# A transformer block with a hand-written order per engine: more warm-up matmuls, two weight corrections moved to ScalarE, and a new order

## The chip, the cores and the metric

The kernel runs on one core of a Trainium2 chip. The metric is device microseconds of one execution. A run is also profiled once: the hardware profiler records every instruction of one execution, and its "span" is the time from the first to the last instruction.

## The reference

One block on x of 2048 rows and 640 columns, in bfloat16: linear attention with 32 heads of 20 columns, then a gated bilinear layer.

```python
q, k, v = split(layernorm(x) @ wqkv)             # 32 heads, Dh = 20
pq = q @ w_phi[h];  pk = k @ w_phi[h]            # 20 x 20 per head
phi_q = concat(softmax(pq), softmax(-pq))        # 40 per head
phi_k = concat(softmax(pk), softmax(-pk))
kv = phi_k^T @ v;  z = sum over rows of phi_k
o = (phi_q @ kv) / (phi_q @ z + 1e-6)
h = x + o @ wo
h2 = h + ((layernorm(h) @ w_gate) * (layernorm(h) @ w_up)) @ w_down
```

## The kernel before, in words

The 2048 rows are 16 tiles of 128. The program is built by a small recorder (`Prog`): every operation names its engine, the regions that it reads and writes, and a unit such as k7. The table `ORDER` (L58 to L107) then gives, for each of PE, DVE, ACT, POOL and SP (the queue that issues DMAs), the sequence of units. Each engine executes its operations strictly in that sequence. `place()` (L205) walks the five lists with planner costs (`t`, `lat`, `at`) to choose buffers and to count semaphores; the costs set no time on the chip and do not change an engine's sequence. Most matmuls write one of four PSUM buffers, so a matmul group also waits until an earlier group's buffer has been read.

The units that matter here, with PE's work and what follows it:

- **warm** (L576): 30 matmuls of 128 columns on a constant, which have no use as arithmetic.
- **wk** (L676): for each of the five row blocks of the key weights, five matmuls of one column (column sums of the weights, for their means) and five transposes through PE. The blocks arrive by three loads: block 0, blocks 1 and 2 (both on SP), blocks 3 and 4 (on ACT's queue). DVE then makes the negative means (L689, `nmean`), POOL spreads them over a tile (L691), and DVE and ACT add them to the transposed blocks (L716, L713).
- **x0 to x4** (L743 to L752): key weights times `Phi`, a band matrix that holds w_phi, in six matmuls each (twice for x0 and x1: once on the raw weights, once on the spread means). DVE builds three fifths of `Phi` (L552) and POOL the rest. ACT (L763) or DVE (L766) copies the product to `Wp`. These are the key weights of all later steps.
- **s0, s2, s4, s8, s12**: row sums and row sums of squares for the layernorm of tiles 0 to 1, 2 to 3, 4 to 7 and so on, from PE; DVE (L613, L617) takes them out of PSUM, POOL makes the scales (`rs`). For s12 ACT takes the squares (L565).
- **wv, c0 to c4**: the sums of the value weights, and DVE's subtraction of their mean (L785).
- **wm, wq0 to wq4, y0 to y4**: the same for the query weights. `lwq` loads the weights, t0 to t4 load their five column blocks transposed (`WT[:, 0]`) by DMA; wm (L726) makes the means on PE and ACT (L730, `nmeanq`); wq (L734) adds the negative means to each of the five blocks, on DVE; y (L737) multiplies by `Phi`.
- **k, v, q**: projections of a tile, ten matmuls of 320 columns each. For a key tile DVE takes the absolute maximum (L815), scales it (L818), ACT does two exponentials (L822); K: DVE sums and inverts (L833, L835), POOL divides (L836). For q the steps are alike (Q: L855, L860, L861, L866), with a transposing DMA behind them.
- **A0 to A14**: kv of two tiles each; **Aout**: DVE takes kv out of PSUM (L902, L905).
- **n, h, f, d, e**: per tile the numerator and division (n), the output projection (h), and per block of four tiles the gated layer up (f) and down (d, e). For tiles 0 and 1 the transposes in n and h go through PE and ACT (L482, L485), for the others by DMA.

The loads of SP's list are called lT (x transposed), lx (x as it is), lwq, lwo, lg, lu, ld.

Of the kernel before, what the change touches and what calls it, by code (L numbers as in the profile page):

```python
# [7 lines left out]
ACT = mybir.ActivationFunctionType  # L8
ALU = mybir.AluOpType
# [38 lines left out]
NRAW = 2  # L48
# [8 lines left out]

ORDER = {  # L58
# [14 lines left out]
    "DVE":  # L73
# [12 lines left out]
    "ACT":  # L86
# [9 lines left out]
    "POOL":  # L96
# [10 lines left out]
}  # L107
# [270 lines left out]
def _build(ctx, nc, A_x, A_wqkv, A_w_phi, A_wo, B_w_gate, B_w_up, B_w_down, out):  # L378
    g = Prog(nc, ctx)
# [43 lines left out]
    nmeanq = sb([P, NC], FP32, "nmeanq")  # L423
# [9 lines left out]
    WT = pq[:, NC * D:3 * NC * D].rearrange("p (w a n) -> p w a n", w=2, a=NC)  # L433
# [18 lines left out]
    R_Wnat, R_WT, R_Phi = regs(NC), [regs(NC), regs((NRAW + 1) * NC)], regs(NC)  # L452
    R_Wp = [regs(NC) for _ in range(3)]
    R_Wrows, R_G, R_id, R_one = Reg(), regs(NC), Reg(), Reg()
    R_Wo, R_Wgu, R_Wd = regs(NC), regs(2), Reg()
    R_wsum, R_nmean, R_nmu, R_nmuk = regs(NC), regs(NC), Reg(), Reg()
# [38 lines left out]
    def U(name):  # L495
        g.unit = name
# [3 lines left out]
    def load_wnat(w, cs=(0, NC), eng="SP", at=0.0):  # L500
        c0, c1 = cs
        load(Wnat[:, c0:c1, :], A_wqkv[P * c0:P * c1, D * w:D * (w + 1)].rearrange("(c p) n -> p c n", p=P), R_Wnat[c0:c1],
             0.3 * (c1 - c0), eng=eng, at=at)
# [8 lines left out]
        load(Wp[:, c0:c1, 2 * D:3 * D], A_wqkv[P * c0:P * c1, 2 * D:3 * D].rearrange("(c p) n -> p c n", p=P), R_Wp[2][c0:c1], 0.16 * (c1 - c0), at=at)  # L512

    U("in")
    load_wnat(1, (3, 5), "ACT", at=4.8)
    load(Wrows[:, :, :], A_w_phi.rearrange("h d f -> (h d) f").rearrange("(a p) f -> p a f", p=P), [R_Wrows], 0.03, eng="ACT", at=5.5)
    load_wnat(1, (0, 1), at=2.9)
    load_wnat(1, (1, 3), at=4.7)
    load_xT(0, 5.35)
    load_xT(1, 5.95)  # L520
    load_wv(0, 5, 9.15)
    for t, at in ((2, 8.95), (3, 9.55)):
        load_xT(t, at)


# [21 lines left out]
    for a in range(NC):  # L547
        lo, hi = CH[a]
        n = hi - lo + 1
# [26 lines left out]
    def warm(n):  # L576
        v = Buf(p_ps, 2)
        one = nc.const_aps.tensor(1.0, (P, P), BF16)
        g.op("PE", lambda e: mms(e, [(PS[v.i][:, 0, 0:P], one, one, True, True) for _ in range(n)]),
             wr=v.R, use=[v], t=0.1 * n, lat=0.1 * n + 0.15)  # L580

# [60 lines left out]
    def wk_rounds():  # L642
        vr, vt = Buf(p_ps, 2), Buf(p_ps, 2)
# [12 lines left out]
        def turn(c):  # L656
            def f(e):
                ins = None
                for a in range(NC):
                    o_ = raw(c)[:, a, :] if c < NRAW else late(a, P * (c - NRAW), P * (c - NRAW + 1))  # L660
                    ins = e.transpose(out=o_, in_=Wnat[:, c, P * a:P * (a + 1)], identity=ident[:, :])  # L661
                return ins
            g.op("PE", f, rd=[R_Wnat[c], R_id], wr=[vr.R[c]] if c < NRAW else vt.R + [vr.R[0]], use=[vr] if c < NRAW else [vt, vr], t=0.28, lat=0.43)

        def means(c):
            v = vx[1]
# [18 lines left out]
        for c in range(NC):  # L685
            U("wk")
            means(c)
            if c == NC - 1:
                g.op("DVE", lambda e: e.tensor_scalar(out=nmean[:, :], in0=PS[vx[1].i][:, 1, MC:MC + NC], scalar1=-1.0 / SC, scalar2=None,  # L689
                                                      op0=ALU.mult), rd=[R_mean], wr=R_nmean, use=[vx[1]], t=0.08, lat=0.2)  # L690
                g.op("POOL", lambda e: e.tensor_copy(nmuk[:, :, :], nmean[:, :].unsqueeze(2).to_broadcast([P, NC, P])), rd=R_nmean,  # L691
                     wr=[R_nmuk], t=0.85, lat=0.95)
# [33 lines left out]
    def wq_means():  # L726
        U("wm")
        v = Buf(p_ps, 2)
        g.op("PE", lambda e: mms(e, mean_mms(PS[v.i][:, 0, :], range(NC), 0)), rd=R_Wnat + [R_one], wr=v.R, use=[v], t=0.64, lat=0.79)
        g.op("ACT", lambda e: e.activation(out=nmeanq[:, :], in_=PS[v.i][:, 0, 0:NC], func=ACT.Copy, scale=-1.0 / SC),  # L730
             rd=[v.R[0]], wr=[R_nmu], use=[v], t=0.1, lat=0.23)
        for a in range(NC):
            U("wq%d" % a)
            g.op("DVE", lambda e, a=a: e.tensor_scalar(out=WT[:, 0, a, :], in0=WT[:, 0, a, :], scalar1=nmeanq[:, a:a + 1], scalar2=None,  # L734
                                                       op0=ALU.add), t=0.35, lat=0.47, rd=[R_nmu, R_WT[0][a]], wr=[R_WT[0][a]])

    def wq_round(i):  # L737
        U("y%d" % i)
# [290 lines left out]
        transpose(lambda: WT[:, 0, a, :], lambda: A_wqkv[:, P * a:P * (a + 1)], [], [R_WT[0][a]], t=1.5, size=0.75, lat=2.75)  # L1029

    U("warm")
    warm(30)
    U("wk")
    wk_rounds()
    for t in range(4, NT):
# [77 lines left out]
```

## Time and profile before

| | us |
|---|---|
| time, median of 3 (280.88 to 282.19) | 281.85 |
| the profiled execution's own time | 281.99 |
| its span | 280.3 |
| PE busy | 275.5 |
| DVE busy | 166.5 |
| ACT busy | 133.6 |
| POOL busy | 107.5 |

Busy time of PE is modelled and runs from the first to the last matmul of a dense stream, so a stall of some 0.1 to 0.3 us between two matmuls of a stream does not show as idle time. It shows in the starts: a group of ten matmuls of 320 columns that follows another starts 1.36 us after it when nothing waits. The timeline gives a start, a duration and a count for each merged group; the idle time in brackets is that of the engine just before the group, with what ended it.

### The profile page before, as it was taken

The numbers are of one execution on the slowest core, as the hardware profiler recorded it, in microseconds if no ns is written. First come the engines' busy times: TensorE is split into PE (matmuls) and PEld (weight loads), VectorE is DVE, ScalarE is ACT, GpSimd is POOL, SyncE is SP. The second block draws the span as 40 slices with busy tenths as digits, with TensorE's granted clock in tenths as the row PEclk, the third lists the DMA queues.
The fourth block names the chain that finished last, engine by engine and source line by source line (L and its number), as shares of the span: only waits on it lengthen the run. The fifth ranks groups of instructions, "written<-read, shape, count | busy, mean of one in ns | idle before, by whom it ended". The sixth has DMA issues, their size and how long they took to land.

```text
span 280.3 us, 5482 instructions
## 1 busy us (share of the span) xinstructions
PE 275.5 (98%) x2231; PEld 187.3 (67%) x2231; DVE 166.5 (59%) x316; ACT 133.6 (48%) x227; POOL 107.5 (38%) x158
## 2 busy tenths in 40 slices
PE   7999999999999999999999999999999999999996
PEld 7967777678868888877756555776454444447773
DVE  2699999999999987588446654404250323324011
ACT  2449998999746564413754513113144224340132
POOL 6636689999823240052140822240300000250151
DMA  7999800149844537978734022446411000000112
GB/s 186 283 239 179 174 4 2 24 104 287 339 96 94 93 75 198 240 114 197 101 79 110 26 47 48 117 96 73 116 23 26 0 0 0 2 23 23 49 47 70
DMA packets 65192, 28.06 MB, mean 100 GB/s; under 512 B 55696, under 2 KB 63888, under 8 KB 65168
## 3 DMA queue, kind: packets, MB, share of 16 engines
q1 hardware_dynamic: 64240, 27.37, 43.4%
q10 hardware_dynamic: 928, 0.35, 0.5%
q8 instruction: 17, 0.28, 0.4%
q14 instruction: 7, 0.06, 0.1%
HBM read 11.82 MB, written 2.62 MB: 52 GB/s over the span
## 4 chain that ended last, share of the span: by engine, by line
PE 96%; DMA 2%; DVE 0%; ACT 0%; SPq 0%; issue 0%
PE ps L572 95%; DMA phiqT<-in_A_wqkv_dram 2%; PE ps L661 1%; PE ps L482 0%; DVE outb L1019 0%; ACT phik L485 0%; SPq L467 0%
## 5 line engine op out<-in xcount | busy, mean ns | idle before, releaser
L572 PE MATMUL ps<-phik,Wgu 128*128 128x512 bf16 (+1 forms) x600 | 107.3, 336 | 0.0
L572 PEld LDWEIGHTS ps<-phik,Wgu 128*128 128x128 bf16 x600 | 58.2, 98 | 43.5 <-DVE phik L978 1.8
L572 PE MATMUL ps<-Wp,xT 128*128 128x320 bf16 x480 | 69.6, 299 | 0.0
L978 DVE TENSOR_TENSOR phik<-ps,gate 128x512 bf16<-128x512 f32 (+1 forms) x60 | 33.9, 578 | 55.6 <-PE ps L572 50.7
L572 PE MATMUL ps<-vaug,phik 128*128 128x320 bf16 (+3 forms) x544 | 60.1, 270 | 0.0
L572 PEld LDWEIGHTS ps<-Wp,xT 128*128 128x128 bf16 x480 | 45.6, 98 | 18.3 <-ACT phik L822 0.5
L976 ACT ACTIVATE gate<-ps 128x512 bf16<-128x512 f32 (+1 forms) x60 | 29.6, 511 | 58.0 <-PE ps L572 40.2
L572 PEld LDWEIGHTS ps<-vaug,phik 128*128 128x128 bf16 x544 | 43.7, 97 | 15.7
L994 POOL TENSOR_TENSOR outb<-t,x_all 128x640 bf16<-128x640 f32 x12 | 16.8, 1396 | 58.0 <-ACT t L991 49.9
L836 POOL TENSOR_TENSOR phik<-phik,Rk 128x1280 bf16<-128x1280 bf16 x16 | 37.4, 2361 | 3.4 <-DVE nb L818 3.4
L991 ACT ACTIVATE t<-ps,mh,rs 128x640 f32<-128x640 f32 x12 | 10.6, 883 | 37.7 <-PE ps L572 37.7
L815 DVE TENSOR_REDUCE ps<-ps 128x1 f32<-128x640 f32 x32 | 25.9, 817 | 1.1 <-PE ps L572 1.0
L855 DVE TENSOR_REDUCE Sq<-eq 128x64 f32<-128x1280 bf16 x16 | 23.5, 1476 | 2.8 <-ACT eq L822 2.7
L822 ACT ACTIVATE eq<-ps,nb,rs 128x640 bf16<-128x640 f32 x16 | 14.1, 884 | 19.7 <-DVE nb L818 13.6
L833 DVE TENSOR_REDUCE Ssum<-phik 128x64 f32<-128x1280 bf16 x16 | 23.2, 1461 | 0.0
L861 POOL TENSOR_TENSOR rq<-Sq,rq 128x32 f32<-128x32 f32 x16 | 4.0, 253 | 47.2 <-DVE rq L860 47.2
L961 POOL TENSOR_SCALAR vpe<-shc 128x1 f32<-128x1 f32 x16 | 3.0, 190 | 45.8 <-ACT junk L565 44.7
L866 POOL TENSOR_TENSOR eq<-eq,rq 128x640 bf16<-128x640 bf16 x16 | 20.2, 1269 | 0.9
L565 ACT ACTIVATE junk<-x_all 128x640 bf16<-128x640 bf16 x20 | 14.6, 733 | 4.4 <-DVE x_all L955 4.4
L822 ACT ACTIVATE phik<-ps,nb,rs 128x640 bf16<-128x640 f32 x16 | 14.2, 885 | 3.3 <-DVE nb L818 3.1
L936 DVE RECIPROCAL rden<-ps 128x32 f32<-128x32 f32 (+1 forms) x18 | 5.6, 324 | 14.7 <-PE ps L572 14.5
L842 ACT ACTIVATE vaug<-ps,rs 128x640 bf16<-128x640 f32 x16 | 12.8, 798 | 3.0 <-PE ps L572 2.9
(85 smaller groups left out, 247.0 us busy)
## 6 DMA issues: line engine op xcount, KB each, us to landing
x_all<-in_A_x_dram SPq DMA_DIRECT2D x4, 640.0 KB, 5.1
out_dram<-outb SPq DMA_DIRECT2D x15, 160.0 KB, 1.8
Wgu<-in_B_w_up_dram SPq DMA_DIRECT2D x1, 1920.0 KB, 9.4
Wgu<-in_B_w_gate_dram SPq DMA_DIRECT2D x1, 1920.0 KB, 15.0
vaug<-in_B_w_down_dram SPq DMA_DIRECT2D x1, 1920.0 KB, 10.3
Wp<-in_A_wqkv_dram SPq DMA_DIRECT2D x1, 800.0 KB, 5.1
phiqT<-in_A_wqkv_dram SPq DMA_DIRECT2D x1, 800.0 KB, 5.3
Wo<-in_A_wo_dram SPq DMA_DIRECT2D x1, 800.0 KB, 4.9
```

The source lines that it names most:

```text
L565: g.op("ACT", lambda e: e.activation(out=junk[:, v.i, :], in_=in_, func=func, accum_out=acc), rd=rd, wr=wr, use=[v], t=0.73, lat=0.97)
L572: ins = e.matmul(o_, lhsT=l_, rhs=r_, start=s_, stop=p_, skip_group_check=True)
L815: g.op("DVE", lambda e: e.tensor_reduce(out=mx(), in_=PS[v.i][:, :, 0:HALF], axis=AX.XY, op=ALU.max, apply_absolute_value=True, negate=Tru ...
L822: g.op("ACT", lambda e, s=s, sc=sc: e.activation(out=signed(dst(), s), in_=PS[v.i][:, :, 0:HALF].rearrange("p b (h f) -> p b h f", f=DH), ...
L833: g.op("DVE", lambda e: e.tensor_reduce(out=Ssum[:, vs.i, :], in_=x, axis=AX.X, op=ALU.add), rd=R_phik[t], wr=vs.R, use=[vs], t=1.39, lat=1.5)
L836: g.op("POOL", lambda e: e.tensor_tensor(out=x, in0=x, in1=Rk[:, vr.i, :].unsqueeze(2).to_broadcast([P, 2 * H, DH]), op=ALU.mult), rd=vr.R ...
L842: g.op("ACT", lambda e: e.activation(out=vaug[:, t, :, 0:DH].rearrange("p (b h) d -> p b h d", b=2), in_=PS[v.i][:, :, 0:HALF].rearrange(" ...
L855: g.op("DVE", lambda e: e.tensor_reduce(out=Sq[:, vs.i, :], in_=eq[:, b.i, :].rearrange("p (g f) -> p g f", f=DH), axis=AX.X, op=ALU.add), ...
L866: return e.tensor_tensor(out=x, in0=x, in1=rq[:, vr.i, :].unsqueeze(2).to_broadcast([P, H, DH]), op=ALU.mult)
L976: g.op("ACT", lambda e: e.activation(out=gate[:, vg.i, 0:P * n], in_=PS[v.i][:, 0, 0:P * n], func=ACT.Copy), rd=[v.R[0]], wr=vg.R, use=[v, ...
L978: g.op("DVE", lambda e: e.tensor_tensor(out=hhT[:, hb, ft, sl], in0=PS[v.i][:, 1, 0:P * n], in1=gate[:, vg.i, 0:P * n], op=ALU.mult), rd=[ ...
L994: g.op("POOL", lambda e: e.tensor_tensor(out=outb[:, vo.i, :], in0=t32[:, v3.i, :], in1=x_all[:, t, :], op=ALU.add), rd=v3.R + [R_h[t]], w ...
```

## The change

`warm(30)` becomes `warm(38)`. Of the five additions of the query weights' means, a = 1 and a = 3 become an ACT activation (Identity with a bias) in place of a DVE addition. Planner costs and due times change (not shown beyond one line). `ORDER` is new up to about the end of the first up-layer block; from there (q12 on PE) it is as before.

```diff
-    warm(30)
+    warm(38)
...
+            if a in (1, 3):
+                g.op("ACT", lambda e, a=a: e.activation(out=WT[:, 0, a, :], in_=WT[:, 0, a, :], func=ACT.Identity, bias=nmeanq[:, a:a + 1]),
+                     t=0.66, lat=0.8, rd=[R_nmu, R_WT[0][a]], wr=[R_WT[0][a]])
+                continue
...
-            g.op("PE", f, rd=[R_Wnat[c], R_id], ... t=0.28, lat=0.43)
+            g.op("PE", f, rd=[R_Wnat[c], R_id], ... t=0.54 if c < 3 else 0.28, lat=0.6 if c < 3 else 0.43)
```

The start of each engine's list, before (-) and after (+), cut where the lists go on:

```diff
 PE
-warm wk wk wk wk wk wk wk wk wk wk x1 s0 s0 x0 x0 x3 x2 x1 wv wv x4 k0 s2 k0 k0 s2 k0 k0 k3 k1 v2 k2 s4 s4 s4 s4 k7 v1 v3 wm k4 v4 k6 v7 y1
+warm wk wk wk wk wk wk wk wk wk s0 wk s0 x1 x1 x3 wv wv x2 x0 x0 s2 s2 x4 k0 k0 k0 k0 k0 k3 k2 wm k1 v1 s4 s4 s4 s4 k6 k4 v5 v0 k7 y3
 PE, around Aout
-A8 A10 A8 A12 A10 A12 A14 A14 q4 n1 n0 n0 n1 q7 n1 n0 h1 h0 n2 q6 h0 h1 n3 q8
+A6 A8 A8 A10 A10 A12 A14 A12 A14 n1 n0 n0 n1 q7 n1 q4 n0 h1 h0 n2 q6 h0 h1 n3 q8
 DVE
-wk in in in wk wk wk wk s0 s0 s0 x3 x1 c1 c3 c0 s2 k0 s2 s2 k0 c4 c2 k3 K0 k3 k1 K0 k2 k1 s4 s4 k2 s4 s4 s4 K3 k7 K3 k7 K1 K2 k4 K2 k4 wq4 wq1 wq0 wq2 wq3
+wk in wk in in wk wk wk s0 x1 s0 x3 s0 c4 c0 c2 s2 c1 s2 s2 k0 k0 c3 k3 k2 k3 K0 k2 k1 K3 k1 s4 s4 s4 s4 s4 wq2 k6 K3 k4 k6 K1 k4 wq0 K1 wq4
 ACT
-in in in wk wk wk x0 x2 x4 k0 k0 v2 k3 k3 k1 k1 k2 k2 v1 s12 wm v3 k7 k7 s12 v4 k4 k4
+in in in wk wk wk x2 x0 x4 k0 k0 wm k3 k3 k2 k2 v1 k1 k1 wq3 wq1 k6 k6 v0 v5 k4 k4
 POOL, the keys' divisions
-K3 K0 K1 K2 K4 K7 ... K6 K5 ... K9 ... K8 K10 K11 K13 K12 K14 K15
+K3 K1 K0 K6 K2 K4 ... K7 ... K5 ... K10 K8 K14 K9 K11 K13 K12 K15
 SP
-in x7 lx3 lT4 lT6 lT5 lT7 lwq t0 t2 t3 t4 lT8 t1 lwo lT10 lT14 lT9 lT12 lT11 lT15 lT13 Q1 Q0 lx0 Q0 Q1 lu lg
+in x7 lwq lT6 lT5 lT4 t2 lT7 t3 t1 t0 t4 lx3 lT11 lT10 lT8 lT9 lT15 lT14 lT12 lT13 lu lwo Q1 Q0 Q0 Q1 lx0 lg
```

More of the change, by code (lines that the diff above doesn't have):

```diff
@@ L514, in _build @@
     U("in")
-    load_wnat(1, (3, 5), "ACT", at=4.8)
+    load_wnat(1, (3, 5), "ACT", at=4.3)
     load(Wrows[:, :, :], A_w_phi.rearrange("h d f -> (h d) f").rearrange("(a p) f -> p a f", p=P), [R_Wrows], 0.03, eng="ACT", at=5.5)
     load_wnat(1, (0, 1), at=2.9)
-    load_wnat(1, (1, 3), at=4.7)
+    load_wnat(1, (1, 3), at=5.05)
     load_xT(0, 5.35)
@@ L521, in _build @@
     load_wv(0, 5, 9.15)
-    for t, at in ((2, 8.95), (3, 9.55)):
+    for t, at in ((2, 9.1), (3, 9.8)):
         load_xT(t, at)
@@ L579, in warm @@
         g.op("PE", lambda e: mms(e, [(PS[v.i][:, 0, 0:P], one, one, True, True) for _ in range(n)]),
-             wr=v.R, use=[v], t=0.1 * n, lat=0.1 * n + 0.15)
+             wr=v.R, use=[v], t=0.107 * n, lat=0.107 * n + 0.15)
     def stats(i0, n):
@@ L662, in f @@
                 return ins
-            g.op("PE", f, rd=[R_Wnat[c], R_id], wr=[vr.R[c]] if c < NRAW else vt.R + [vr.R[0]], use=[vr] if c < NRAW else [vt, vr], t=0.28, lat=0.43)
+            g.op("PE", f, rd=[R_Wnat[c], R_id], wr=[vr.R[c]] if c < NRAW else vt.R + [vr.R[0]], use=[vr] if c < NRAW else [vt, vr], t=0.54 if c < 3 else 0.28,
+                 lat=0.6 if c < 3 else 0.43)
         def means(c):
@@ L733, in wq_means @@
             U("wq%d" % a)
+            if a in (1, 3):
+                g.op("ACT", lambda e, a=a: e.activation(out=WT[:, 0, a, :], in_=WT[:, 0, a, :], func=ACT.Identity, bias=nmeanq[:, a:a + 1]),
+                     t=0.66, lat=0.8, rd=[R_nmu, R_WT[0][a]], wr=[R_WT[0][a]])
+                continue
             g.op("DVE", lambda e, a=a: e.tensor_scalar(out=WT[:, 0, a, :], in0=WT[:, 0, a, :], scalar1=nmeanq[:, a:a + 1], scalar2=None,
-                                                       op0=ALU.add), t=0.35, lat=0.47, rd=[R_nmu, R_WT[0][a]], wr=[R_WT[0][a]])
+                                                       op0=ALU.add), t=0.55, lat=0.67, rd=[R_nmu, R_WT[0][a]], wr=[R_WT[0][a]])
     def wq_round(i):
```

64 rows, old and new, of the table ORDER are left out of this document.

## The prediction, made before the run

> **What bounds the kernel now.** I read the page first, then the windows, then the chain in order of time.
>
> ```profile
> PE 275.5 (98%) x2231; PEld 187.3 (67%) x2231; DVE 166.5 (59%) x316; ACT 133.6 (48%) x227; POOL 107.5 (38%) x158
> PE 96%; DMA 2%; DVE 0%; ACT 0%; SPq 0%; issue 0%
> ```
>
> PE bounds the whole kernel: the chain that ends last is 96% PE. So a microsecond that PE loses anywhere is lost at the end, and one that it saves counts only if no other engine makes it wait afterwards. The windows (busy time of PE, weight loads, DVE, ACT, POOL, then granted clock) show who could:
>
> ```profile
> 0.00:10.00 10.00, 8.51 (x102) 8.28 (x103) 3.01 (x10) 3.24 (x5) 5.22 (x27) 1.00 0.90 229
> 20.00:40.00 20.00, 19.96 (x208) 15.21 (x207) 19.92 (x42) 18.59 (x30) 13.13 (x13) 1.00 0.76 137
> 20.00:70.00 50.00, 49.96 (x494) 37.43 (x493) 49.52 (x96) 46.81 (x76) 42.46 (x39) 1.00 0.52 112
> ```
>
> From 20 to 70 us DVE is full, ACT 94% and POOL 85%, with most of POOL's idle time before 40. So the change can gain in the first 10 us, where PE is idle or slow, and it can lose anything behind them, where DVE is as full as PE.
>
> **The start, step by step.** The timeline of the first 13 us:
>
> ```profile
> 0.83 3.36 PE L572 MATMUL ps<-const-bfloat16-1.0 128*128 128x128 bf16 x30 [0.83 <-PEq L1098]
> 3.98 0.32 PE L572 MATMUL ps<-ones,phiqT 128*128 128x1 bf16 x5
> 5.51 0.29 PE L572 MATMUL ps<-ones,phiqT 128*128 128x1 bf16 x5 [0.66 <-DMA phiqT<-in_A_wqkv_dram]
> 5.71 1.20 DVE L552 TENSOR_TENSOR Phi<-Wrows,G 128x140 bf16<-128x140 bf16 x3 [0.33 <-DMA Wrows<-in_A_w_phi_dram]
> 7.67 0.69 PE L661 MATMUL ps<-ident,phiqT 128*128 128x128 bf16 x5
> 7.84 0.17 DVE L689 TENSOR_SCALAR nmean<-ps 128x5 f32<-128x5 f32 x1 [0.93 <-PE ps L572]
> 8.15 0.81 PE L572 MATMUL ps<-Phi,phiqT 128*128 128x140 bf16 x6
> 8.40 1.07 DVE L716 TENSOR_SCALAR phiqT<-ps,nmean 128x384 bf16<-128x384 bf16 x3 [0.39 <-PE ps L661]
> 8.75 1.13 PE L572 MATMUL ps<-xT 128*128 128x129 bf16 x10
> 9.72 0.48 PE L572 MATMUL ps<-Phi,phiqT 128*128 128x140 bf16 x6
> 10.03 0.48 PE L572 MATMUL ps<-Phi,outb 128*128 128x140 bf16 x6
> 13.07 0.43 PE L572 MATMUL ps<-Wp,xT 128*128 128x320 bf16 x2
> ```
>
> Thirty warm-ups take 3.98 - 0.83 = 3.15 us, 0.105 each. Eight more put the first wk round at 4.82. The chain gives a round's pace:
>
> ```profile
> 1.25 4.22 DMA phiqT<-in_A_wqkv_dram
> 6.36 0.11 PE ps L572 x5
> 6.47 0.56 PE ps L661 x5
> ```
>
> A round is 0.11 + 0.56 = 0.67 us, so the first ends at 5.49, and the second round's data lands at 1.25 + 4.22 = 5.47. So **the eight warm-ups cost nothing**: they fill the wait before 5.51. If that load came earlier they would cost up to 0.84 us.
>
> What they buy is pace. Six x matmuls take 8.75 - 8.15 = 0.60 us, the next six 10.03 - 9.72 = 0.31. The ten of s0 take 0.97 us, at nearly half the pace of the twenty of s4 (22.01 - 20.77 = 1.24, rows below). So PE's pace doubles late in s0; with eight matmuls at 0.107 and two at 0.06 that is near 9.6. The granted clock of the stretch reads 1.00 and does not show it. PE had worked without a break for 3.8 us (0.83 to 4.65) and was still slow; after the break it worked 4.1 us (5.51 to 9.6) and became fast. The new start has no long break after 0.83. Bounds for the doubling are then 0.83 + 4.1 = 4.9 and 9.6 as now; I take 4.9, from the one unbroken stretch that the rows show.
>
> The Trainium skill, "TensorE: Matmul & The Clock Gate", Part 1, says otherwise: a free-running window of some 3.4 us must be busy before the clock doubles. Windows ending at 2.8, 6.2 and 9.6 agree with the rows (the middle one holds the wait, the last is full), and by the same phase the start below would gain 0.7 instead of 0.9; by the phase alone, which the Trainium skill calls variable from run to run, 0.2 to 0.9.
>
> With the doubling at 4.9 a round takes about 0.42 (half of 0.56, and 0.14 for the sums). Round 1 ends before 5.47, rounds 2 to 4 at 5.93, 6.35 and 6.77. The new order puts half of s0 ahead of the last transposes: last sums at 6.91 (now 7.67), last transposes at 7.48 (now 8.15), s0 done at 7.77. Then DVE limits. Its new list does one `Phi` product before the means and two behind them (1.20 / 3 each, the wide one longer: 0.85): means 7.08 to 7.25, `Phi` to 8.10, additions (1.07) to 9.17; now they end at 9.47. So x1's two products run at 8.15 to 8.8, x3 starts at 9.2, and PE idles some 0.8 us in between. The value weights must have landed for wv:
>
> ```profile
> 4.38 0.59 SPq L467 DMA_DIRECT2D Wp<-in_A_wqkv_dram  x1
> 5.01 2.53 SPq L471 DMA_TRANSPOSE xT<-in_A_x_dram  x2
> Wp<-in_A_wqkv_dram SPq DMA_DIRECT2D x1, 800.0 KB, 5.1
> xT<-in_A_x_dram SPq DMA_TRANSPOSE x16, 4.4
> ```
>
> They land at 4.38 + 5.1 = 9.48, just ahead of wv at 9.51. Then wv 1.36 (ten matmuls of 320, the pace below), x2, x0, x0 0.93, s2 0.57 from 11.8 (its second tile lands at about 6.3 + 4.4 = 10.7), x4 0.31: k0 starts at 12.68 and ends at 14.04. Now k0 starts at 13.07 with both halves of s2 inside: 13.07 + 1.36 + 0.57 = 15.0. **The start gains 0.9 us** (bounds: 0 with the doubling at 9.6; nothing beyond 0.95, since the landing of the value weights is next).
>
> The Trainium skill, "TensorE: Matmul & The Clock Gate", Part 4, says that transposes do not count as PE work for the clock, which would leave the doubling where it is. The trace disagrees: rounds 3 to 5 spent 3 x 0.56 = 1.7 of the last 3.4 us before 9.6 on transposes, and the pace doubled.
>
> **The key stage, 14 to 76 us.** Here the 0.9 us must survive.
>
> ```profile
> 20.77 1.30 PE L572 MATMUL ps<-xT 128*128 128x129 bf16 x20
> 22.01 4.25 PE L572 MATMUL ps<-Wp,xT 128*128 128x320 bf16 x30
> 26.09 0.77 PE L572 MATMUL ps<-ones,phiqT 128*128 128x1 bf16 x25
> 32.30 0.49 PE L572 MATMUL ps<-Phi,phiqT 128*128 128x140 bf16 x6
> 29.84 2.40 DVE L734 TENSOR_SCALAR phiqT<-phiqT,nmeanq 128x640 bf16<-128x640 bf16 x5
> L565 ACT ACTIVATE junk<-Wo 128x640 bf16<-128x640 bf16 x5 | 3.7, 748 | 0.0
> L833 DVE TENSOR_REDUCE Ssum<-phik 128x64 f32<-128x1280 bf16 x16 | 23.2, 1461 | 0.0
> ```
>
> A projection is (26.09 - 22.01) / 3 = 1.36 us. The new place of y3 comes after nine of them, wm (0.63) and s4 (1.24): 14.05 + 12.25 + 1.9 = 28.2. It needs all five wq. An addition on DVE is 2.40 / 5 = 0.48 us, so **DVE is relieved of 0.96 us**. On ACT the trace has no such operation; the bounds are the copies of this size, 0.70 to 0.80 us, and I take 0.75 from the row with the same tile and types: **ACT is loaded with 1.5 us**, and has 1.4 us idle from 20 to 40 us. When are the wq done? Up to its last wq, DVE's new list is shorter by one key sum (1.46), two additions (0.96), one subtraction of the value means and one reciprocal (0.8 and 0.5), and two squares moved ahead of k0 (0.4): 4.1 us. Now they end at 29.84 + 2.40 = 32.24; so 28.1, against PE at 28.2. It fits, with nothing to spare. In both orders DVE starts on k0's maximum at about 15. On ACT the wq wait for `nmeanq` and for t3 and t1, and behind them stand k6's exponentials, whose PSUM buffer k7 needs: 1.5 us later than without them, at about the time when PE comes to k7 (26.8). That is the tightest place.
>
> SP issues a tile in 1.27 us and a t in 1.46:
>
> ```profile
> 14.41 0.58 SPq L467 DMA_DIRECT2D phiqT<-in_A_wqkv_dram  x1
> 15.04 5.84 SPq L471 DMA_TRANSPOSE phiqT<-in_A_wqkv_dram  x4
> phiqT<-in_A_wqkv_dram SPq DMA_TRANSPOSE x5, 4.8
> ```
>
> lwq moves from 14.41 to about 7.7 (it overwrites what the last transposes read, at 7.48). Behind it come T6, T5, T4, t2, T7, t3, t1, t0, t4: T7 is issued at 13.6 and lands, after the median 4.4, at 18.0, while s4 comes at 14.05 + 5.4 + 0.6 = 20.1; t1 is issued at 16.3 and lands at 21.1, t4 at 19.2 and 24.0, both before their wq. lx3 falls from 7.6 to 20.7; its first reader on ACT stands behind v4 now. Wo goes behind the up weights, its first reader behind k9. I cost SP's order at 0: T7 has 2 us of cover, t4 some 4.
>
> POOL must finish the keys before A14.
>
> ```profile
> 58.23 16.25 POOL L836 TENSOR_TENSOR phik<-phik,Rk 128x1280 bf16<-128x1280 bf16 x7
> 75.93 1.52 PE L572 MATMUL ps<-Wp,xT 128*128 128x320 bf16 x10
> 75.75 0.58 DVE L902 TENSOR_TENSOR KVsb<-ps,Gk 128x400 bf16<-128x400 f32 x1 [0.18 <-PE ps L572]
> 77.02 0.23 DVE L905 SCALAR_TENSOR_TENSOR KVsb<-ps,Gk 128x20 bf16<-128x20 f32 x1
> 79.62 0.68 PEld L482 LDWEIGHTS ps<-ident,ob 128*128 128x128 bf16 x10 [0.37 <-DVE ob L938]
> 80.87 2.58 PEld L572 LDWEIGHTS ps<-Wo,phik 128*128 128x128 bf16 x20 [0.57 <-ACT phik L485]
> ```
>
> It ends at 74.48 now; A14 with its last group runs up to 75.9, so 0.8 us are in hand even if POOL gains nothing.
>
> **Around Aout** q4 moves. Now it covers DVE's 1.5 us on kv (75.75 to 77.25); then PE waits 0.37 and 0.57 us for the transposes of tiles 0 and 1. After the change q4 stands between those transposes, which hides the 0.57 and the later half of the division; but n1 now follows A14 directly, and only one group of A12 and A14 (0.8 us) covers the first half of kv. That leaves about 0.4 us of waits before q7 and 0.2 before each transpose: 0.8 against 0.9. I take **0.1 gained**, bounds -0.9 and +0.5. The rest, from 88 us on, has the same work and a list that soon is the same word for word: 0.
>
> **The sum.** 281.99 (the profiled execution, 0.14 above the median) less 0.9 and 0.1 gives 281.0.
>
> **The rivals.**
>
> *More than that.* DVE is so far ahead at Aout that kv and the division make nobody wait, and the two waits there (0.37 + 0.57) go: 281.99 - 0.9 - 0.9 = 280.2. For it: DVE, the fullest engine, is relieved of 0.96 us and starts earlier. Against: kv cannot start before A14 has ended, however free DVE is.
>
> *The gain is swallowed.* PE reaches k7 or A14 sooner, but the buffer (ACT's extra 1.5 us) or POOL is not sooner, and PE waits there what it won: 282.0. For it: ACT idles only 3.2 us of the 50 from 20 to 70, POOL 0.7 from 40 on. Against: POOL idles 6.9 us between 20 and 40, ACT 1.4.
>
> *The clock is not lifted sooner*, so the warm-ups do not do what they are there for: the rounds keep their times, and s0 ahead of the last transposes and the late `Phi` delay x3 to about 10.1, where PE now has done x0: 282.0 to 282.3. The Trainium skill's sentence on transposes ("TensorE: Matmul & The Clock Gate", Part 4) would bring this; the rows speak against it.
>
> *Slower: y3 stands too early.* It decides if the last wq ends later than 28.2 + 0.9 us; beyond that each microsecond costs one. If DVE is only its 0.96 us ahead of now, the last wq ends at 31.3, PE waits 3.1 us, and the time is 281.0 + 3.1 = 284.1. For it: y3 comes 4.1 us sooner than y1 now (32.30), and the list of a full engine must match that. Against: the listed 4.1 us.
>
> **How the numbers follow.** Chances: forecast 0.45, more 0.20, swallowed 0.13, no lift 0.07, slower 0.15. A measurement can tell about 0.5% from no change, which is 280.4 and 283.3 here. Faster by that: 0.14 of "more" and 0.08 of the forecast's lower tail, 0.22. Slower: 0.14. Within: 0.64. The range 279.8 to 282.8 holds all but most of the slower case and the ends of "more".
>
> **What would show it.** First wk sums at 4.8; five transposes in about 0.28 us from the second round on; k0's end at 14.05; wq on ACT near 0.75 us and y3 without a wait at 28; n1 waiting for DVE's L905; h1 at about the same distance from A14 as now. The forecast is wrong if all rounds keep 0.67 us, or if PE idles over 0.5 us between 25 and 45 us.

## The result, and the profile after

| | before | after |
|---|---|---|
| median, one comparison, 22 runs each (us) | 281.07 | 280.68 |
| lowest to highest | 280.69 to 282.30 | 280.45 to 280.99 |
| profiled execution, and its span | 281.99, 280.3 | 280.50, 278.8 |

The ratio is 0.9981 with a 95% interval of 0.9972 to 0.9989: 0.4 us faster, within what the prediction called the same. The forecast was 281.0.

**The times of before stand in two groups.** Of 113 executions of it in this study 60 lie between 280.53 and 281.35 and 53 between 281.54 and 282.39. The changed kernel has one group. The execution that the prediction read, 281.99, is of the upper group. So profile against profile the change is worth 1.5 us, and median against median 0.4; both have to be explained.

The page of the changed kernel, first the span, the busy times and the chain's shares:

```profile
span 278.8 us, 5485 instructions
...
PE 273.6 (98%) x2227; PEld 186.8 (67%) x2239; DVE 166.2 (60%) x314; ACT 135.3 (49%) x229; POOL 107.3 (38%) x158
...
PE 95%; DMA 2%; DVE 1%; issue 0%; SPq 0%
```

PE still bounds the whole. ACT has 1.7 us more and DVE only 0.3 less, although two operations went from one to the other. Now the changed kernel's timeline at the start (start, duration, group; in brackets the idle time ahead):

```profile
0.82 4.21 PE L572 MATMUL ps<-const-bfloat16-1.0 128*128 128x128 bf16 x38 [0.82 <-PEq L1103]
4.83 0.32 PE L572 MATMUL ps<-ones,phiqT 128*128 128x1 bf16 x5
...
5.73 0.44 PE L661 MATMUL ps<-ident,phiqT 128*128 128x128 bf16 x5
...
6.13 0.44 PE L661 MATMUL ps<-ident,phiqT 128*128 128x128 bf16 x5
...
8.39 0.48 PE L572 MATMUL ps<-Phi,phiqT 128*128 128x140 bf16 x6 [0.18 <-DVE Phi L552]
...
9.28 0.49 PE L572 MATMUL ps<-Phi,phiqT 128*128 128x140 bf16 x6
9.61 1.52 PE L572 MATMUL ps<-Wp,ones 128*128 128x320 bf16 x10
...
12.87 3.30 PE L572 MATMUL ps<-Wp,xT 128*128 128x320 bf16 x23
```

A round of sums and transposes takes 6.13 - 5.73 = 0.40 us, where it took 0.67. From one matmul's start to the next, the pace doubles at 5.11, in the first round's transposes; in the profiled execution of before that was near 9.6. k0 starts at 12.87 with both halves of s2 done.

Three points that both lists share divide the time: k0's first matmul, the last matmul of A14, the first of the up layer. The last two come from the timeline around them. Of the changed kernel, nine A matmuls from 74.33 (0.038 apart, so the last starts at 74.64), and the up layer:

```profile
74.33 0.51 PE L572 MATMUL ps<-vaug,phik 128*128 128x84 bf16 x9
...
86.36 0.71 PE L572 MATMUL ps<-phik,Wgu 128*128 128x256 bf16 x5
```

The same of the kernel before, profiled execution (fourteen from 75.40, the last at 75.90):

```profile
75.40 0.69 PE L572 MATMUL ps<-vaug,phik 128*128 128x84 bf16 x14
...
87.86 0.60 PE L572 MATMUL ps<-phik,Wgu 128*128 128x256 bf16 x4
```

| us | before, profiled | after, profiled | difference | predicted |
|---|---|---|---|---|
| up to k0, with s2 (0.57 added to before) | 13.64 | 12.87 | -0.77 | -0.9 |
| k0 to the last A matmul (0.57 off before) | 62.26 | 61.77 | -0.49 | 0 |
| from there to the up layer | 11.96 | 11.72 | -0.24 | -0.1 |
| the rest, to PE's last matmul | 189.41 | 189.42 | 0 | 0 |

The sum is -1.50, against 281.99 - 280.50 = 1.49 measured. The forecast had -1.0.

### The profile page after: what moved, and what is told of

It is laid out like the page before. It is cut to its first block, busy times and chain, and to the rows that moved or that the text cites. A ratio compares the mean times of both kernels' runs of the same rounds, so it can differ in the third digit from the quotient of the medians.

```text
span 278.8 us, 5485 instructions
## 1 busy us (share of the span) xinstructions
PE 273.6 (98%) x2227; PEld 186.8 (67%) x2239; DVE 166.2 (60%) x314; ACT 135.3 (49%) x229; POOL 107.3 (38%) x158
## 4 chain that ended last, share of the span: by engine, by line
PE 95%; DMA 2%; DVE 1%; issue 0%; SPq 0%
PE ps L572 95%; DMA phiqT<-in_A_wqkv_dram 2%; PE ps L482 0%; DVE outb L1024 0%; DVE phiqT L717 0%; PE ps L661 0%; DVE Phi L552 0%; DVE KVsb L907 0%; SPq L467 0%; DVE nmean L690 0%; DVE KVsb L910 0%; DVE sm L613 0%; DVE nb L823 0%
## 5 line engine op out<-in xcount | busy, mean ns | idle before, releaser
L572 PE MATMUL ps<-phik,Wgu 128*128 128x512 bf16 (+1 forms) x589 | 105.9, 336 | 0.6
L572 PE MATMUL ps<-Wp,xT 128*128 128x320 bf16 x480 | 68.6, 299 | 0.0
L983 DVE TENSOR_TENSOR phik<-ps,gate 128x512 bf16<-128x512 f32 (+1 forms) x60 | 33.8, 575 | 56.0 <-PE ps L572 51.2
L827 ACT ACTIVATE phik<-ps,nb,nrs 128x640 bf16<-128x640 f32 x16 | 14.2, 885 | 0.0
```

Source lines behind the costliest of these rows:

```text
L572: ins = e.matmul(o_, lhsT=l_, rhs=r_, start=s_, stop=p_, skip_group_check=True)
L827: g.op("ACT", lambda e, s=s, sc=sc: e.activation(out=signed(dst(), s), in_=PS[v.i][:, :, 0:HALF].rearrange("p b (h f) -> p b h f", f=DH), ...
L983: g.op("DVE", lambda e: e.tensor_tensor(out=hhT[:, hb, ft, sl], in0=PS[v.i][:, 1, 0:P * n], in1=gate[:, vg.i, 0:P * n], op=ALU.mult), rd=[ ...
```

## The experiments

Each kernel is compared with executions of before on the same chip. A ratio takes in both groups of before, so it does not equal the ratio of two medians.

**b_again**: the kernel before, unchanged.

> The kernel before, unchanged, for a second profile. Its 22 times stand in two groups, 280.7 to 281.2 and 281.7 to 282.3, and the profile shown is of the upper one (281.99). Theory 1 (the doubling of PE's pace comes at a moment that varies from run to run, early or late, because the wait before the second wk round breaks the unbroken work): a profile of the lower group shows the doubling before 9.6 us and its first key projection about 1 us sooner than 13.07; the times again stand in two groups, median about 281.0. Theory 2 (the groups come from something behind the start, such as DMA landings): the start is the same as before to 0.2 us and the difference lies behind 15 us.

Measured: median 281.86, from 280.74 to 282.36; ratio 0.9993 (0.9974 to 1.0011). Five of its twelve runs are at most 281.03, seven at least 281.63. The two groups belong to the kernel and not to one comparison. The profiled execution is again of the upper group (282.10, k0 at 13.06), so it cannot yet tell the two theories apart.

**b_warm38**: only the warm-ups.

```diff
-    warm(30)
+    warm(38)
```

> The kernel before with 38 warm-ups and nothing else. Theory 1 (the warm-ups are what the start gains by, and the new order of the start is not needed for it): the doubling falls near 5.1 us as in the changed kernel, the last transposes end near 7.4 instead of 8.15, k0 starts 1.0 to 1.5 us sooner than 13.07, no time lies above 281.3, and the median is 0.3 to 0.8 us under that of before. Theory 2 (the new order makes the gain, the warm-ups alone nothing): the median is within 0.15 us of before.

Measured: 280.84, from 280.74 to 281.18; ratio 0.9970 (0.9956 to 0.9984). The upper group is gone. Its pace doubles at 5.18 and k0 starts at 11.97.

**a_warm30**: the changed kernel with the 30 warm-ups of before.

```diff
-    warm(38)
+    warm(30)
```

> The changed kernel with 30 warm-ups again. Theory 1: the wait before the second round comes back (0.66 us), the doubling is late in some runs, two groups of times come back, median 0.3 to 1.0 us over the changed kernel (281.0 to 281.7). Theory 2: the new order alone keeps the whole gain, 280.6 to 280.8, in one group.

Measured: median 280.72; ratio 0.9975 (0.9959 to 0.9990). Two groups again: seven runs from 280.44 to 280.75, five from 281.42 to 281.73. The profiled one is of the upper group. Its timeline:

```profile
4.16 0.69 PE L661 MATMUL ps<-ident,phiqT 128*128 128x128 bf16 x5
5.60 0.29 PE L572 MATMUL ps<-ones,phiqT 128*128 128x1 bf16 x5 [0.75 <-DMA phiqT<-in_A_wqkv_dram]
...
9.33 0.81 PE L572 MATMUL ps<-Phi,phiqT 128*128 128x140 bf16 x6
9.93 0.57 PE L572 MATMUL ps<-Phi,outb 128*128 128x140 bf16 x6
...
13.96 1.26 PE L572 MATMUL ps<-Wp,xT 128*128 128x320 bf16 x8
```

The wait for the second load is back, six matmuls still take 9.93 - 9.33 = 0.60 us, the pace doubles at 10.11, and k0 starts 1.1 us later than in the changed kernel. That is about the distance between its groups, 280.61 and 281.50 by their medians.

In the same comparison the groups of before have their medians at 280.88 and 282.14, and the one group of b_warm38 at 280.84. So the warm-ups take the upper group away and leave the lower one where it was; the new order is worth some 0.3 us in the lower group and 0.6 in the upper.

**b_look** and **b_look2**: the kernel before again, one profiled execution each, to have one of the lower group.

> The kernel before, unchanged, one more look for a profile of its lower group of times. Theory 1: if the time is below 281.3, PE's pace doubles before 5.2 us and k0 starts about 1.1 us sooner than 13.06; if it is above 281.6, the doubling is near 9 to 10 us.

> The kernel before, unchanged, once more. Theory 1: if its time is below 281.3, the profile shows the doubling of PE's pace before 5.2 us, as with 38 warm-ups, and a first key projection near 12; if it is above 281.6, the doubling is near 9 to 10 us and the first key projection near 13.1 to 13.3, as in the three profiles so far.

The first took 282.29 and had the slow start (k0 at 13.27). The second took 280.82. Its timeline, with the 30 warm-ups and the wait:

```profile
4.16 0.48 PE L661 MATMUL ps<-ident,phiqT 128*128 128x128 bf16 x5
5.65 0.28 PE L572 MATMUL ps<-ones,phiqT 128*128 128x1 bf16 x5 [1.01 <-DMA phiqT<-in_A_wqkv_dram]
...
12.02 0.43 PE L572 MATMUL ps<-Wp,xT 128*128 128x320 bf16 x2
```

The first round's transposes take 0.48 instead of 0.69: the pace doubled at 4.28, before the wait. The wait is even longer than in the upper group (1.01 against 0.75 in a_warm30's), so neither a late load nor the wait's length makes the groups. What differs is whether the doubling comes before the wait or some 5 us later. From k0 on the two executions run alike (62.85 in b_look2 and 62.83 in the one that the prediction read, to the last A matmul).

**a_warm46**: eight more warm-ups still.

```diff
-    warm(38)
+    warm(46)
```

> The changed kernel with 46 warm-ups. Theory 1 (38 just fill the wait for the second load, and what goes beyond pushes the chain of means, Phi, additions and x3): the first round starts at 5.68, the second at about 6.1 instead of 5.59, the time is 0.3 to 0.6 us over the changed kernel. Theory 2 (DVE's Phi products or the landing of the value weights cover it): within 0.15 us.

Measured: 280.84, from 280.50 to 281.42; ratio 0.9973 (0.9959 to 0.9988). In the profiled execution, 281.39 and the second slowest of the twelve, the first round starts at 5.68 and the second at 6.24 instead of 5.59:

```profile
5.68 0.31 PE L572 MATMUL ps<-ones,phiqT 128*128 128x1 bf16 x5
...
6.24 0.27 PE L572 MATMUL ps<-ones,phiqT 128*128 128x1 bf16 x5
```

There k0 starts at 13.74, 0.87 later than in the changed kernel, and that execution is 0.89 longer, so it paid for the rounds' delay of 0.65 in full. By the ratios the twelve together cannot be told from the changed kernel (0.9981): neither theory is settled, and no gain from more than 38 warm-ups is shown.

**a_wq_dve**: all five query additions on DVE, the two from ACT right behind wq4, the last that y3 needs.

```diff
-            if a in (1, 3):
+            if a in ():
 DVE
-... k4 wq0 K1 wq4 K0 ...
+... k4 wq0 K1 wq4 wq1 wq3 K0 ...
```

> The changed kernel with all five additions of the query weights' means on DVE, the two of ACT put right behind wq4 in DVE's list. Theory 1 (the last addition sets when y3 can start, and PE pays for each later microsecond): they end 0.6 to 1.0 us later, PE waits that long at y3 (28.5 us), and the time is 0.4 to 1.0 us over the changed kernel, 281.1 to 281.7. Theory 2 (DVE has room and PE finds other work behind): within 0.2 us of the changed kernel.

Measured: 285.38; ratio 1.0134 (1.0112 to 1.0155), 4.7 us more than the changed kernel, where neither theory expected more than 1.0. The timelines of DVE, POOL and PE:

```profile
28.31 3.58 DVE L739 TENSOR_SCALAR phiqT<-phiqT,nmeanq 128x640 bf16<-128x640 bf16 x3
...
28.46 2.35 POOL L841 TENSOR_TENSOR phik<-phik,Rk 128x1280 bf16<-128x1280 bf16 x1 [0.72 <-DVE Rk L840]
30.76 0.66 POOL L560 MEMSET vaug<- 128x128 bf16 x1
...
31.94 0.78 PE L572 MATMUL ps<-Phi,phiqT 128*128 128x140 bf16 x6 [3.18 <-DVE phiqT L739]
```

Three additions take 3.58 us. By the row of their line (shortest, median and longest in ns), one of them takes 3085 ns:

```profile
L739 DVE TENSOR_SCALAR phiqT<-phiqT,nmeanq x5: 280/384/3085, 22.7 to 31.5; 128x640 bf16<-128x640 bf16 x5
```

It started at 28.51, 0.05 after POOL's division, and ended at 31.60, 0.18 after POOL's memset (30.76 + 0.66 = 31.42). PE, which needs all five, starts y3 at 31.94 instead of 28.48. Then comes a second loss; the windows of the same kernel (busy time and count of PE, weight loads, DVE, ACT, POOL; then the granted clock):

```profile
28.00:31.40 3.40, 0.77 (x6) 0.32 (x4) 3.40 (x3) 2.26 (x4) 2.94 (x2) 1.00 1.12 156
31.40:34.80 3.40, 2.86 (x15) 1.94 (x16) 3.40 (x7) 0.00 (x0) 2.37 (x2) 0.50 0.67 128
34.80:38.00 3.20, 3.20 (x29) 2.37 (x28) 2.92 (x4) 2.80 (x4) 0.00 (x0) 1.00 0.91 233
```

After the wait PE works at half pace: the granted clock is 0.50 from 31.39 to 34.80, and matmuls of 320 columns start 0.267 us apart in place of 0.136. From k0 to the last A matmul the kernel takes 66.34 against 61.77: 3.46 for the wait and 1.11 for the half pace.

**a_wq_early**: all five on DVE too, but the two right behind wq2, where POOL has no division.

```diff
-... s4 wq2 k6 ... wq0 K1 wq4 wq1 wq3 K0 ...
+... s4 wq2 wq3 wq1 k6 ... wq0 K1 wq4 K0 ...
```

> The changed kernel with all five additions on DVE as in a_wq_dve, but the two of ACT put directly behind wq2 in DVE's list (at about 22.6 us, when POOL runs only short operations) and not behind wq4. Theory 1 (a DVE addition of this kind cannot run while POOL runs a key division of 2.35 us: in a_wq_dve one took 3.1 us and ended with POOL's division and the memset behind it, alone one takes 0.28 to 0.38): each takes under 0.7 us, no wait over 1 us at y3, the time is within 0.6 us of the changed kernel, 280.5 to 281.3. Theory 2 (DVE's load as such is what cost a_wq_dve 4.7 us: two more operations ahead of y3): again over 283.

Measured: 280.79, from 280.46 to 281.03; ratio 0.9979 (0.9963 to 0.9994). The timeline of DVE:

```profile
22.74 0.97 DVE L739 TENSOR_SCALAR phiqT<-phiqT,nmeanq 128x640 bf16<-128x640 bf16 x3
...
27.02 1.05 DVE L739 TENSOR_SCALAR phiqT<-phiqT,nmeanq 128x640 bf16<-128x640 bf16 x1
...
28.46 0.28 DVE L739 TENSOR_SCALAR phiqT<-phiqT,nmeanq 128x640 bf16<-128x640 bf16 x1
```

Three additions in 0.97 us, and the time of the changed kernel. So ACT is not what the two needed. They needed a place away from POOL's long operations, and ACT is one such place.

**a_phi**: the third `Phi` product of DVE ahead of the means again.

```diff
-wk in wk in in wk wk wk s0 x1 s0 x3 ...
+wk in in in wk wk wk wk s0 x1 s0 x3 ...
```

> The changed kernel with DVE's three Phi products ahead of the means, as in the kernel before, instead of one ahead and two behind. Theory 1 (PE's idle 0.8 us between s0 and x3 comes from the two late products): the additions end at about 8.7 instead of 9.2, x3 starts at about 8.8, k0 0.2 to 0.5 us sooner than 12.87 (the value weights land at 9.35 and bound wv), the time 0.1 to 0.4 us under the changed kernel. Theory 2 (the landing of the value weights, or DVE at y3, takes it back): k0 or y3 waits what x3 won, the time within 0.1 us of the changed kernel.

Measured: 280.54, all but one of twelve from 280.33 to 280.74; ratio 0.9977 (0.9959 to 0.9995). PE's timeline:

```profile
8.05 0.48 PE L572 MATMUL ps<-Phi,phiqT 128*128 128x140 bf16 x6
...
9.17 0.48 PE L572 MATMUL ps<-Phi,phiqT 128*128 128x140 bf16 x6 [0.32 <-DVE sm L613]
...
12.74 1.53 PE L572 MATMUL ps<-Wp,xT 128*128 128x320 bf16 x10
```

x1 starts 0.34 sooner, but x3 only 0.11 (9.17 against 9.28) and k0 0.13. x3 waits for DVE's additions, which now wait for the last transposes:

```profile
7.97 1.07 DVE L717 TENSOR_SCALAR phiqT<-ps,nmean 128x384 bf16<-128x384 bf16 x3 [0.73 <-PE ps L661]
```

So the place of that `Phi` product is worth about 0.13 us, too little for these intervals to show by itself.

**a_q4back**: in the changed kernel, q4 between A14 and n1 as before.

```diff
 PE
-... A14 A12 A14 n1 n0 n0 n1 q7 n1 q4 n0 h1 ...
+... A14 A12 A14 q4 n1 n0 n0 n1 q7 n1 n0 h1 ...
 DVE
-... n0 n0 q7 n0 q7 Q5 q4 h1 Q5 h1 h0 q4 h0 n2 n2 ...
+... n0 n0 q4 n0 q7 q4 Q5 h1 Q5 h1 q7 h0 h0 n2 n2 ...
 ACT
-n1 n0 q7 q7 q4 q4
+n1 n0 q4 q4 q7 q7
```

> The changed kernel with q4 back between A14 and n1 on PE, and q4 ahead of q7 on DVE and ACT there, as in the kernel before. Theory 1 (the new place is worth about 0.1 to 0.3 us: it hides ACT's copy of the transposes and uncovers DVE's 1.5 us on kv): n1 no longer waits for kv, h1 waits about 0.6 us for ACT, the time is 0.0 to 0.4 us over the changed kernel. Theory 2 (the stage has slack on both sides): equal to 0.05 us.

Measured: 281.69; ratio 1.0014 (0.9998 to 1.0029), some 0.9 above the changed kernel's 0.9981, more than the 0.0 to 0.4 expected. From the last A matmul to the up layer it takes 12.48 against 11.72. Its timeline, with the weight loads, which wait first:

```profile
78.29 0.93 PE L572 MATMUL ps<-KVsb,phiqT 128*128 128x84 bf16 x20
79.72 1.20 PEld L572 LDWEIGHTS ps<-Wp,xT 128*128 128x128 bf16 x10 [0.64 <-ACT eq L827]
...
81.88 0.28 PEld L482 LDWEIGHTS ps<-ident,ob 128*128 128x128 bf16 x5 [0.51 <-DVE ob L943]
```

q4 hides the kv as it did, but q7 then waits for a PSUM buffer that ACT's exponentials of an earlier tile still read, and a transpose waits 0.51 us for DVE's division. (The profiled execution, 283.54, also lost 1.8 us at the start, where its value weights landed late; the stage is read alone for that reason.)

**a_best**: a_phi with wq0 and wq4 put ahead of POOL's division as well.

```diff
-... s4 wq2 k6 K3 k4 k6 K1 k4 wq0 K1 wq4 K0 ...
+... s4 wq2 k6 wq0 wq4 K3 k4 k6 K1 k4 K1 K0 ...
```

> The changed kernel with the Phi products as in a_phi, and the DVE additions wq0 and wq4 put ahead of K3's reciprocal, so that they run before POOL's first key division. Theory 1 (the addition that took 1.15 us behind POOL's division falls to 0.3 to 0.4 and PE no longer waits 0.2 to 0.3 us near 26.7 and 28.4): 0.2 to 0.5 us under the changed kernel, 0.0 to 0.3 under a_phi. Theory 2 (PE is bound by buffers there, not by the additions): equal to a_phi to 0.05 us.

Measured: 281.09, from 280.71 to 283.51; ratio 0.9994 (0.9975 to 1.0013). It fell short of a_phi by 0.5. PE's timeline:

```profile
21.40 5.60 PE L572 MATMUL ps<-Wp,xT 128*128 128x320 bf16 x40
27.70 1.53 PE L572 MATMUL ps<-Wp,xT 128*128 128x320 bf16 x10 [0.70 <-ACT phik L827]
```

The two additions were short (0.38 and 0.39, the second after 0.28 of waiting for its load), but k6's and k4's steps on DVE stood behind them, so ACT's exponentials of k6 came later (25.98, against 25.35 in the changed kernel) and k7 waited for their PSUM buffer. It is the place that the prediction called the tightest: 0.2 us are lost there in the changed kernel (the pace at 26.7 shows 0.34 from one matmul to the next instead of 0.14), 0.86 here.

## Why the prediction was right, and where it was not

The forecast of 281.0 is 0.3 from the median, and its sum is 0.5 from the profiled execution. That it came so near is in part luck: the same terms, taken off an execution of the lower group (280.82 in b_look2), would have given 279.8, 0.9 under the median. By its steps:

- **"The eight warm-ups cost nothing"** held: the second round starts at 5.59, where its load lands (1.25 + 4.29 = 5.54). By the ratios they alone do as much as the whole change (0.9970 and 0.9981, with intervals that overlap); what the new order adds shows only when group is compared with group, as under a_warm30.
- **"PE's pace doubles" at 4.9, "from the one unbroken stretch that the rows show"**: the size was close (5.11), the rule was not. The doublings in the changed kernel and its variants came at 4.00 (a_wq_early), 4.08 (a_wq_dve), 5.11 (also a_phi), 6.53 (a_best) and 6.82 (a_q4back), with the same 38 warm-ups from 0.82. And in a_wq_dve 4.08 + 8 x 3.413 = 31.38, where the pace halved, and it lasted 3.41; in the changed kernel the granted clock falls to 0.50 behind the last matmul, at 278.18, which is 5.11 + 80 x 3.4133 (278.18). So there is a grid of 3.41 us whose phase is another in each execution. The Trainium skill, "TensorE: Matmul & The Clock Gate", Part 1, gives such a free-running window of 4096 cycles or 3413 ns, and these rows agree with it to 0.01 us. The prediction named that rule and set it aside for a start that the rule explains better.
- **The base.** "Its own time" of 281.99 was taken as the kernel's time. It is the time of an execution whose pace doubled late; b_look2, whose pace doubled at 4.28, takes 280.82. The prediction called the phase variable from run to run and applied that only to the gain, not to the time that it subtracted from. The three times shown, 280.88 to 282.19, were both groups. This is why 1.5 us by the profiles are 0.4 by the medians.
- **"The start gains 0.9 us"**: 0.77 against the upper group. Against the lower one it loses 0.3 (12.02 + 0.57 = 12.59 in b_look2, 12.87 now), and against b_warm38, at the same pace, too (12.54). The prediction saw PE's idle time between s0 and x3 and counted it, but had no fast start with the old order to compare it with. DVE's two `Phi` products behind the means are part of it: a_phi gets 0.13 of 0.33 back. For the rest the traces point to the half of s0 that the new order puts ahead of the last transposes: these start at 6.95 in b_warm38 and at 7.49 in a_phi, and DVE's additions, for which x3 waits, at 7.43 and at 7.97. That place was not tried by itself.
- **"DVE is relieved of 0.96 us", at 0.48 an addition**: the mis-sized term. The 0.48 was a mean over unequal ones. In the kernel before, by the row of their line, one of the five took 1.21 us and the others some 0.37:

```profile
L734 DVE TENSOR_SCALAR phiqT<-phiqT,nmeanq x5: 368/374/1212, 29.8 to 31.9; 128x640 bf16<-128x640 bf16 x5
```

  In the changed kernel the three that remain take 1.81 us together, 0.6 less than the 2.40 of the five; in DVE's timeline, with the key sum for comparison:

```profile
22.55 0.38 DVE L739 TENSOR_SCALAR phiqT<-phiqT,nmeanq 128x640 bf16<-128x640 bf16 x1
...
25.16 1.48 DVE L838 TENSOR_REDUCE Ssum<-phik 128x64 f32<-128x1280 bf16 x1
...
26.61 1.15 DVE L739 TENSOR_SCALAR phiqT<-phiqT,nmeanq 128x640 bf16<-128x640 bf16 x1
...
28.15 0.28 DVE L739 TENSOR_SCALAR phiqT<-phiqT,nmeanq 128x640 bf16<-128x640 bf16 x1
```

  and POOL's timeline has the reason for the middle one:

```profile
25.22 2.36 POOL L841 TENSOR_TENSOR phik<-phik,Rk 128x1280 bf16<-128x1280 bf16 x1
```

  The addition of 26.61 ends 0.18 after that division (25.22 + 2.36 = 27.58). Alone an addition takes 0.28 to 0.38; started beside a division it lasts until POOL lets go. The key sum beside the same division takes its usual 1.48 and is not held up. The Trainium skill, "SBUF — State Buffer", under "Who interferes with whom", says that a VectorE operation in a two-port mode and a GpSimd operation share a port pair that one of them holds for its whole instruction; the additions agree with that, up to 3.09 us behind two POOL operations in a row. That a move of the two, on DVE or to ACT, takes the block away was shown; the port itself is the page's explanation and was not measured apart.
- **"It fits, with nothing to spare"** held: the last addition ends at 28.15 + 0.28 = 28.43, and y3 starts at 28.48 without a wait (forecast 28.2). The slower rival was the right one to fear: a_wq_dve, which ends its last addition at 31.9, is the rival's case and costs 3.46 us for the wait, where it had 3.1, and 1.1 more for the pace.
- **ACT "loaded with 1.5 us"** at 0.75 each: 0.72 from the start of one to the start of the next, 0.86 for one, 1.57 for the two in its timeline.

```profile
23.38 1.57 ACT L736 ACTIVATE phiqT<-phiqT,nmeanq 128x640 bf16<-128x640 bf16 x2
```

- **The key stage at 0** was 0.49 too high. In the profiled execution of before, six pairs of matmuls there (at 16.2, 17.7, 21.8, 32.0, 36.2 and 50.6) start 0.1 to 0.2 us further apart than their pace, 0.87 in all; after, two do (26.7 and 33.8), 0.39 in all. The section on the profile before says that such stalls show only in the starts, and the prediction's sum left them out. Which part of the new order removed which of them was not tried.
- **"0.1 gained" around Aout** was 0.24, and the place of q4 alone is worth more, 0.76 in the stage by a_q4back. "0.2 before each transpose" did not come: the first transposes start right behind q7 (76.05 + 1.36 = 77.41) and the second right behind q4 (77.69 + 1.36 = 79.05). What is left is the wait for kv, 0.25 us ahead of n1, as predicted by name, and 0.37 inside it, in the chain of waits of the changed kernel:

```profile
74.87 0.58 DVE KVsb L907
75.45 0.15 DVE KVsb L910
```

- **SP's order and POOL at 0** held: no PE wait on a load or on POOL's keys stands in the changed kernel between k0 and Aout.
- **The rival "the clock is not lifted", 282.0 to 282.3**: its case is a_warm30's upper group, 281.4 to 281.7; the gains in the key stage and around Aout, which it had at 0 and 0.1, are the difference. The Trainium skill's sentence that transposes do not count as work for the clock ("TensorE: Matmul & The Clock Gate", Part 4) finds no support in these runs: in the kernel before the pace doubled near 9.6 after 3.4 us half of which were transposes.

What stays open: how full a window must be for the pace to double. In a_wq_dve the window from 31.39 to 34.80 sufficed although PE's first matmul in it comes at 31.94, after 0.55 us. In the profiled execution of before the one that by the grid ran from 2.8 to 6.2 did not, with the wait of 0.66 in it. So the bound should lie between, by these two. That would also explain the size of the groups, by an estimate: in before a window that bridges the wait well enough ends between 0.83 + 3.41 less the allowed wait and 4.85 (the end of the first round) plus it, which is 1.7 to 1.9 us of the 3.41, 50 to 57% if every phase is as likely as another; 60 of 113 are 53%. With 38 warm-ups the wait that is left is 0.11 (5.01 + 0.47 = 5.48 to 5.59), under that bound, and the upper group is gone. No run varied the wait alone.

## What to carry to other kernels

Look at the spread of the times before trusting one profile: two groups 1.3 us apart mean that the profiled execution is a draw from one of them, and a change that only removes the worse group looks, profile against profile, like a gain of up to that much. Cover PE's early waits with warm-ups up to the landing of the load; eight more showed no gain here, and the one execution of them that was profiled paid for them. Before an operation is moved from DVE to another engine, read the duration of each of its instances and not their mean: a long one beside a POOL operation may need only another place in DVE's own list.

## What the runs showed of the hardware

- PE's pace doubles and halves on a grid of 3.41 us that does not start with the kernel: doublings at 4.00 to 6.82 with 38 warm-ups, and at 4.28 or at 9.4 (b_again) to 10.1 with 30.
- One wait of 3.5 us (28.47 to 31.94, of which the profile counts 3.18 as idle) put PE back to half pace for 3.41 us, at a cost of 1.1 us, although the 3.4 us before the halving still held 0.77 us of PE's work. Here the granted clock shows it (0.50); at the start, up to the doubling, it reads 1.00 although the matmuls are twice as far apart (0.107 against 0.056 us).
- A DVE addition of 128 x 640 bf16 takes 0.28 to 0.38 us alone, 1.15 when started 1.4 us into a POOL division, and 3.09 when started 0.05 us behind one that a POOL memset follows; a DVE reduce beside the same kind of division is not slowed.
